# Transposing keys and queries by the DMA crossbar instead of by matmuls, in an attention kernel fused with a gated long convolution

## Chip, core and metric

The kernel runs on one core of one Trainium2 chip. The metric is the device time of one execution in microseconds (us); lower is better. Every run has a span (first to last instruction). A single run over 1.5% above the fastest of its kernel counts as slow and is left out of ratios.

## The reference

For 4 batches, 8 heads, 768 positions and a head dimension of 64, each query attends to the 8 first keys and to the 96 last ones, with a slope per head. The result, as a [768 x 512] matrix per batch, is projected to three parts; the second is convolved over the whole sequence, multiplied with the other two, and projected once more.

```python
scores = scale * q @ k.T                  # kept: key < 8, or 0 <= query - key < 96
a = softmax(scores - slope[h] * dist)
x = heads_side_by_side(a @ v)             # [B, 768, 512]
x1, x2, x3 = split(x @ w_proj)
y = x1 * irfft(rfft(x2) * rfft(filter)) * x3
out = y @ w_out                           # float32
```

## The kernel before

The engines' names: PE is TensorE's matmul, PEld its weight load, DVE VectorE, ACT ScalarE, POOL GpSimd, SP SyncE. Keys lie in seven tiles of 128 rows: the 8 global keys, then 120 local ones. POOL issues the loads (float32 to float16 on the way); SP issues a small copy that repeats the 8 global rows in all seven tiles, and the output stores.

```python
def load_tiles(self, dst, src, b):                       # keys or values
    g.dma_start(dst[0:NG, 0, :, 0:D], src[b, :, 0:NG, :]...)
    self.nc.sync.dma_start(dst[0:NG, 1:7], dst[0:NG, 0:1].to_broadcast(...))   # by SP
    for t in range(7):
        g.dma_start(dst[NG:P, t, :, 0:D], src[b, :, lo:lo + KL, :]...)         # by POOL

def load_batch(self, b):
    qt, kt, vt = self.batch_tiles()      # natural layout, two buffers of each
    self.load_tiles(kt, self.k, b)
    for t in range(6):
        g.dma_start(qt[:, t], self.q[b, :, P * t:P * t + P, :]...)
    self.load_tiles(vt, self.v, b)
    if b == 1: ...                       # gate parts of w, then w_out
```

Scores need head dimensions on the partitions. So for each pair of heads PE transposes six blocks of queries and seven of keys against an identity; ACT copies the queries' result out of PSUM, DVE the keys'.

```python
def transpose_k(self, hp, kt, first):    # branch for batches 1 to 3
    for m in range(7):
        nc.tensor.transpose(tk[:, P * m:P * m + P], kt[:, m, hs, :], self.ident)
    nc.vector.tensor_copy(KT, tk[:, 0:7 * P])

def weights(self, hp, gi, QT, KT):       # scores of one pair, one of three groups
    sp = self.ps.tile([P, 2, 512], F32, tag="s", bufs=1)    # a single PSUM buffer
    ...                                  # matmuls of KT and QT into sp
    nc.scalar.activation(eo, sp[...], Act.Exp, scale=self.scale)
```

`weave` records the attention of batch b+1 and the rest (called hyena: projections, transforms, gates, output) of batch b in turns, chunk by chunk. Each engine then runs its instructions in the recorded order. The matmuls meant to keep PE's clock up in batch 0 are idle ones (`busy`).

The softmax here doesn't subtract the row's maximum and nothing guards it: scores larger than these inputs give would overflow.

## Time and profile before

The median was 212.75 us (212.4 to 213.83, four runs). I divide the span at the first matmul of each hyena, the accumulation of the weights' middle part with `xa`:

| stretch of the profile before | from, us | length, us |
|---|---|---|
| batch 0's attention, filter, tables | 0 | 46.08 |
| first middle stage: hyena 0 and attention 1 | 46.08 | 43.17 |
| second middle stage | 89.25 | 43.04 |
| third middle stage | 132.29 | 42.70 |
| last stage: hyena 3 alone | 174.99 | 35.01 |

In order of time PE's row looks so at the start of the second middle stage. The columns are start and length in us, engine, line, operation, output<-inputs, shapes and count; a bracket gives the idle time before and what ended it:

```profile
85.67 3.40 PE L661 MATMUL pt<-wo,y 128*128 128x512 f16 x15
88.91 0.50 PE L466 MATMUL tr<-ident,qt 128*128 128x128 f16 x6
89.25 1.03 PE L579 MATMUL pt<-w,xa 128*128 128x512 f16 x4
90.45 0.55 PE L491 MATMUL tr<-ident,kt 128*128 128x128 f16 x7 [0.18 <-ACT QT L471]
...
91.80 0.36 PE L503 MATMUL sp<-QT,KT 64*128 64x216 f16 x4
```

PE goes from the output projection (`wo`) into the next stage without a gap: the transposes of the new batch stand between matmuls of the other stream, and the first scores (`sp`) come at 91.80. The loads are far ahead. POOL waited 15.0 us for a values buffer before it began batch 3's loads at 83 us, for a stage that starts at 132.

### The profile page before, as it was taken

The page shows a single profiled execution, that of the slowest core. Times are in us where ns is not written, and L with a number is a line of the kernel's source. Part 1 is how long each engine was busy: PE and PEld are TensorE (multiplying, and loading weights), DVE is VectorE, ACT ScalarE, POOL GpSimd, SP SyncE. Part 2 cuts the span into 40 slices and gives each one's busy share as a digit, 9 for nine tenths or more (in the row PEclk, how much of TensorE's full clock was granted, in tenths as well). Part 3 has the DMA queues.
Part 4 walks back from the last instruction along what each step waited for, and adds up shares of the span by engine and source line. Part 5 has one row for each costly group of instructions (what it writes and reads, how often), then busy time and mean ns, then how long its engine had stood idle before and what let it go on. Part 6 is the DMA issues. An engine that isn't in the chain of part 4 may idle for free.

```text
span 210.0 us, 4253 instructions
## 1 busy us (share of the span) xinstructions
PE 189.5 (90%) x1661; PEld 102.7 (49%) x1661; DVE 147.0 (70%) x328; ACT 149.7 (71%) x243; POOL 75.6 (36%) x102
## 2 busy tenths in 40 slices
PE   7587888679899999998999999989999999998981
PEld 2233454345465656444555664535565654454630
DVE  5965899973499999332999995147998960196820
ACT  6997985436797785769786866787859856665642
POOL 7999459995699001996810000000000000000000
PEclk9999999999999999999999999999999999999998
DMA  5999999999999900999990003500000025000034
GB/s 190 167 124 189 205 154 155 126 142 207 158 157 137 81 3 0 147 235 184 143 97 2 3 2 116 186 0 3 0 0 3 2 100 203 0 0 0 3 118 185
DMA packets 79629, 20.62 MB, mean 98 GB/s; under 512 B 71336, under 2 KB 76536, under 8 KB 79608
## 3 DMA queue, kind: packets, MB, share of 16 engines
q0 software_dynamic: 74672, 12.13, 91.8%
q1 hardware_dynamic: 4936, 8.21, 11.6%
q8 instruction: 13, 0.21, 0.4%
q14 instruction: 8, 0.07, 0.1%
HBM read 25.79 MB, written 6.29 MB: 153 GB/s over the span
## 4 chain that ended last, share of the span: by engine, by line
DVE 48%; PE 29%; ACT 8%; issue 5%; DMA 5%; POOL 3%; POOLq 0%; DVEq 0%
DVE xn L540 9%; PE pt L661 7%; PE pt L579 7%; DVE g L570 6%; PE pt L565 4%; DVE E_107 L522 3%; DMA t<-in_k_dram 3%; DMA vt<-in_v_dram 2%; DVE E_107 L519 2%; PE tr L547 2%; DVE rc L539 2%; ACT E_104 L510 2%; DVE y L651 2%; PE tr L491 2%; PE pt L643 2%
## 5 line engine op out<-in xcount | busy, mean ns | idle before, releaser
L565 PE MATMUL pt<-xT,w 128*128 128x384 f16 x256 | 46.5, 327 | 0.0
L565 PEld LDWEIGHTS <-w 128*128 128x128 f16 x256 | 23.3, 98 | 15.9 <-issue 1.6
L107 POOL DMA_DIRECT2D vt<-in_v_dram x28 | 25.7, 944 | 1.4 <-DMA qt<-in_q_dram 0.8
L510 ACT ACTIVATE E_107<-sp 128x864 f16<-128x864 f32 x24 | 21.5, 897 | 2.7 <-PE sp L503 2.7
L510 ACT ACTIVATE E_104<-sp 128x864 f16<-128x864 f32 x24 | 21.6, 899 | 2.2 <-PE sp L503 1.9
L664 ACT ACTIVATE t<-pt 128x512 f32<-128x512 f32 x24 | 14.3, 598 | 12.0 <-PE pt L661 11.8
L107 POOL DMA_DIRECT2D kt<-in_k_dram x21 | 19.0, 915 | 10.3 <-DMA fl<-in_moe_filter_fft_dram 4.2
L503 PE MATMUL sp<-QT,KT 64*128 64x216 f16 (+2 forms) x224 | 17.8, 250 | 5.4 <-ACT E_104 L510 2.5
L661 PE MATMUL pt<-wo,y 128*128 128x512 f16 x96 | 22.0, 379 | 0.7 <-DVE y L654 0.7
L540 DVE TENSOR_TENSOR xn<-o,rc 128x448 f16<-128x448 f32 x32 | 20.0, 624 | 1.1
L548 ACT COPY xT<-tr 128x768 f16<-128x768 f16 x16 | 12.8, 797 | 9.4 <-PE tr L547 9.4
L643 PE MATMUL pt<-inv,X 128*128 128x384 f16 x96 | 18.4, 326 | 0.9 <-DVE X L604 0.9
L503 PEld LDWEIGHTS <-KT 64*128 64x128 f16 x224 | 7.7, 95 | 23.5 <-issue 19.8
L581 ACT CAST dst<-pt 128x512 f16<-128x512 f32 x24 | 14.3, 596 | 6.8 <-PE pt L579 6.8
L327 PE MATMUL pt<-dst,fwd 128*128 128x512 f16 x72 | 18.8, 379 | 0.0
L607 ACT CAST X<-pt 128x512 f16<-128x512 f32 x24 | 14.1, 589 | 6.4 <-PE pt L327 6.0
L522 DVE TENSOR_TENSOR E_104<-E_104,mask 128x864 f16<-128x864 f16 x16 | 9.6, 603 | 9.7 <-ACT E_104 L510 8.8
L115 POOL DMA_DIRECT2D qt<-in_q_dram x18 | 15.9, 903 | 1.3 <-DMA kt<-in_k_dram 1.3
L279 PE MATMUL pt<-idle 128*128 128x512 f16 x35 | 15.1, 436 | 1.3 <-DVE warm L688 1.2
L661 PEld LDWEIGHTS <-y 128*128 128x128 f16 x96 | 8.8, 98 | 10.9 <-DVE y L654 2.1
L492 DVE COPY KT<-tr 128x896 f16<-128x896 f16 x12 | 7.4, 618 | 7.7 <-PE tr L491 7.7
L579 PE MATMUL pt<-w,xa 128*128 128x512 f16 x48 | 12.2, 380 | 0.3 <-DVE xa L450 0.3
(234 smaller groups left out, 370.4 us busy)
## 6 DMA issues: line engine op xcount, KB each, us to landing
out_dram<-t SPq DMA_DIRECT2D x24, 256.0 KB, 2.4
vt<-in_v_dram POOLq DMA_DIRECT2D x28, 120.0 KB, 6.5
kt<-in_k_dram POOLq DMA_DIRECT2D x21, 120.0 KB, 9.1
qt<-in_q_dram POOLq DMA_DIRECT2D x18, 128.0 KB, 5.7
w<-in_moe_w_proj_dram POOLq DMA_DIRECT2D x3, 512.0 KB, 8.0
t<-in_q_dram SPq DMA_DIRECT2D x2, 384.0 KB, 5.8
t<-in_k_dram SPq DMA_DIRECT2D x2, 384.0 KB, 5.6
fl<-in_moe_filter_fft_dram POOLq DMA_DIRECT2D x1, 768.0 KB, 11.9
```

The lines of the kernel that those rows point to most:

```text
L107: g.dma_start(dst[NG:P, t, :, 0:D], src[b, :, lo:lo + KL, :].rearrange("h p d -> p h d"))
L115: g.dma_start(qt[:, t], self.q[b, :, P * t:P * t + P, :].rearrange("h p d -> p h d"))
L279: self.nc.tensor.matmul(pt, self.idle[:, 0:P], self.idle, start=True, stop=True)
L327: self.nc.tensor.matmul(pt, self.fwd[:, kt, s, :], src[:, kt, :], start=(kt == 0), stop=(kt == 2))
L503: nc.tensor.matmul(sp[:, hh, off:off + w], KT[64 * hh:64 * hh + 64, o:o + P], QT[64 * hh:64 * hh + 64, KL * m:KL * m + w], start=(off == 0 ...
L510: nc.scalar.activation(eo, sp[:, :, 0:432].rearrange("p h (m w) -> p h m w", m=2), Act.Exp, scale=self.scale)
L522: nc.vector.tensor_mul(eo, eo, mk[:, :, 0:2] if gi == 0 else mk[:, :, 1:3])
L540: nc.vector.tensor_mul(xn[:, :, hh, :], o[:, :, 0:D], rc.to_broadcast([P, 7, D]))
L565: nc.tensor.matmul(pt[:, 0:h], self.w[:, c, o + P * j:o + P * j + P], xT[:, c, h * s:h * s + h], start=(c == 0), stop=(c == 3))
L579: nc.tensor.matmul(pt, src[:, c, P * t:P * t + P], self.w[:, c, DM:2 * DM], start=(c == 0), stop=(c == 3))
L643: nc.tensor.matmul(pt[:, 0:h], X[:, s, cs], self.inv[:, s, :], start=(s == slots[0]), stop=(s == slots[-1]))
L661: nc.tensor.matmul(pt, y[:, c, P * t:P * t + P], self.wo[:, c, :], start=(c == 0), stop=(c == 3))
```

## The change

The keys of batches 1 to 3 and the queries of 2 and 3 are to be transposed by the crossbar of the DMA, SBUF to SBUF, issued by SP. PE, DVE and ACT lose the work; nothing on them takes its place. The natural keys and queries now have one buffer each instead of two, since the room goes to whole transposed tiles. The queries of batch 1 stay with PE, because the DMA is full at that time (9 tenths busy up to 73 us in the profile before).

```diff
+LATE = 26
+GATES = (1, 0, 0, 0, 1, 0, 3)
     def load_batch(self, b):
+        kt = self.ld.tile([P, 7, H, D], F16, tag="k", bufs=1)
+        qt = self.ld.tile([P, 6, H, D], F16, tag="q", bufs=1)
         self.load_tiles(kt, self.k, b)
         for t in range(6):
             g.dma_start(qt[:, t], self.q[b, :, P * t:P * t + P, :]...)
+        KT, QT = self.transposed_tiles()
+        if b == 1:
+            self.QT1, QT = QT, None
+        def transposed():
+            self.nc.sync.dma_start_transpose(KT..., kt...)          # 28 blocks of 128x128
+            for t in range(6 if QT is not None else 0):
+                self.nc.sync.dma_start_transpose(QT[:, :, t], qt[:, t]...)   # 4 blocks each
+        vt = self.batch_tiles()
+        if b == 1:
+            transposed()
+        else:
+            self.after(LATE, transposed)        # recorded 26 chunks later
         self.load_tiles(vt, self.v, b)
@@ attention: no key transposes, query transposes only for batch 1
-                             (i + 1 < n, lambda: trk(i + 1)),
+                             (i + 1 < n and first, lambda: trk(i + 1)),
-                             (i + 1 < n, lambda: trq(i + 1)),
+                             (i + 1 < n and (first or natural), lambda: trq(i + 1)),
@@ ... batch 0's scratch moves into these tiles; the weave's chunk counts become 29 and 25
```

More of the change, by code (lines that the diff above doesn't have):

```diff
@@ L92, in batch_tiles @@
         D = self.D
-        qt = self.ld.tile([P, 6, self.H, D], F16, tag="q")
-        kt = self.ld.tile([P, 7, self.H, D], F16, tag="k")
         vt = self.ld.tile([P, 7, self.H, D + 1], F16, tag="v")
         self.nc.gpsimd.memset(vt[:, :, :, D:D + 1], 1.0)
-        return qt, kt, vt
+        return vt
     def load_tiles(self, dst, src, b):
@@ L108, in load_tiles, with transposed_tiles @@
                         src[b, :, lo:lo + KL, :].rearrange("h p d -> p h d"))
+    def transposed_tiles(self):
+        KT = self.ld.tile([P, 7, self.H // 2, P], F16, tag="KT")
+        QT = self.ld.tile([P, self.H // 2, 6, P], F16, tag="QT")
+        return KT, QT
     def load_batch(self, b):
         g = self.nc.gpsimd
-        qt, kt, vt = self.batch_tiles()
+        H, D = self.H, self.D
+        kt = self.ld.tile([P, 7, H, D], F16, tag="k", bufs=1)
+        qt = self.ld.tile([P, 6, H, D], F16, tag="q", bufs=1)
         self.load_tiles(kt, self.k, b)
@@ L115, in load_batch @@
             g.dma_start(qt[:, t], self.q[b, :, P * t:P * t + P, :].rearrange("h p d -> p h d"))
+        KT, QT = self.transposed_tiles()
+        if b == 1:
+            self.QT1, QT = QT, None
+        def transposed():
+            self.nc.sync.dma_start_transpose(KT.rearrange("c t a p -> c (t a) p"),
+                                             kt.rearrange("p t h d -> p (t h d)"))
+            for t in range(6 if QT is not None else 0):
+                self.nc.sync.dma_start_transpose(QT[:, :, t],
+                                                 qt[:, t].rearrange("p h d -> p (h d)"))
+        vt = self.batch_tiles()
[3 more added lines that the diff above has]
+            self.after(LATE, transposed)
         self.load_tiles(vt, self.v, b)
@@ L120, in load_batch @@
             self.load_w_out()
-        return qt, kt, vt
+        return QT if QT is not None else qt, KT, vt
     def load_first(self):
@@ L142, in cast_first @@
         for src in (sq, sk):
-            t = self.mp.tile([P, 6, P], F16, tag=f"c{len(out)}", name="t")
+            t = self.cst[:, hp % 2, len(out)]
             self.nc.vector.tensor_copy(t.rearrange("p t (h d) -> p t h d", h=2),
@@ L377, in filter_spectrum, with attention @@
             yield 1
-    def attention(self, qt, kt, vt, xT, xa, xb, first=None):
+    def attention(self, qt, kt, vt, xT, xa, xb, first=None, natural=False):
         n = self.H // 2
         qk, cst = {}, {}
+        if not first:
+            qk = {i: {0: None if natural else qt[:, i].rearrange("c t p -> c (t p)"),
+                      1: kt[:, :, i]} for i in range(n)}
         def trq(i):
-            if i < n:
-                qk.setdefault(i, {})[0] = self.transpose_q(i, cst[i][0] if first else qt, first)
+            qk.setdefault(i, {})[0] = self.transpose_q(i, cst[i][0] if first else qt, first)
         def trk(i):
-            if i < n:
-                qk.setdefault(i, {})[1] = self.transpose_k(i, cst[i][1] if first else kt, first)
+            qk.setdefault(i, {})[1] = self.transpose_k(i, cst[i][1])
         def sc(i, g):
@@ L422, in attention @@
             cst[0], ths = first
-        trq(0)
-        if first:
+            trq(0)
             for a in (2, 3):
                 self.dft_sines(a, ths[a][0])
-        yield 1
-        trk(0)
-        cast(1)
-        yield 1
+            yield 1
+            trk(0)
+            cast(1)
+            yield 1
+        elif natural:
+            trq(0)
+            yield 1
         for i in range(n + 1):
             for live, fn in ((i < n, lambda: sc(i, 0)),
-                             (i + 1 < n, lambda: trk(i + 1)),
+                             (i + 1 < n and first, lambda: trk(i + 1)),
                              (i < n, lambda: sc(i, 1)),
                              (i > 0, lambda: val(i - 1, 0)),
-                             (i + 1 < n, lambda: trq(i + 1)),
+                             (i + 1 < n and (first or natural), lambda: trq(i + 1)),
                              (i > 0, lambda: val(i - 1, 1)),
@@ L460, in transpose_q @@
         nc, S = self.nc, self.S
-        hs = slice(2 * hp, 2 * hp + 2)
-        QT = self.ap_.tile([P, S], F16, tag="qT")
         tq = self.tr(first)
-        src = qt if first else qt[:, :, hs, :]
-        for st in range(6):
-            nc.tensor.transpose(tq[:, P * st:P * st + P], src[:, st], self.ident)
         if first:
+            QT = self.qk[:, hp % 2, 7 * P:]
+            for st in range(6):
+                nc.tensor.transpose(tq[:, P * st:P * st + P], qt[:, st], self.ident)
             nc.scalar.copy(QT.rearrange("c (p r) -> c p r", r=6),
@@ L470, in transpose_q, with transpose_k @@
         else:
+            QT = self.QT1[:, hp].rearrange("c t p -> c (t p)")
+            for st in range(6):
+                nc.tensor.transpose(tq[:, P * st:P * st + P], qt[:, st, 2 * hp:2 * hp + 2, :],
+                                    self.ident)
             nc.scalar.copy(QT, tq[:, 0:S])
         return QT
-    def transpose_k(self, hp, kt, first):
+    def transpose_k(self, hp, kt):
         nc, S = self.nc, self.S
-        hs = slice(2 * hp, 2 * hp + 2)
-        KT = self.ap_.tile([P, 7 * P], F16, tag="kT")
-        tk = self.tr(first)
-        if first:
-            for st in range(6):
-                nc.tensor.transpose(tk[:, P * st:P * st + P], kt[:, st], self.ident)
-            tv = tk[:, 0:S].rearrange("c (r p) -> c p r", r=6)
-            kv = KT.rearrange("c (t j) -> c t j", t=7)
-            loc = kv[:, :, NG:].rearrange("c t (p r) -> c t p r", r=6)
-            nc.vector.tensor_copy(loc[:, 0:6], tv[:, 0:KL].rearrange("c (t p) r -> c t p r", t=6))
-            nc.vector.tensor_copy(loc[:, 6], tv[:, P - 20:P])
-            nc.vector.tensor_copy(kv[:, :, 0:NG],
-                                  kv[:, 0:1, NG:2 * NG].to_broadcast([P, 7, NG]))
-        else:
-            for m in range(7):
-                nc.tensor.transpose(tk[:, P * m:P * m + P], kt[:, m, hs, :], self.ident)
-            nc.vector.tensor_copy(KT, tk[:, 0:7 * P])
+        KT = self.qk[:, hp % 2, 0:7 * P].rearrange("c (t p) -> c t p", t=7)
+        tk = self.tr(True)
+        for st in range(6):
+            nc.tensor.transpose(tk[:, P * st:P * st + P], kt[:, st], self.ident)
+        tv = tk[:, 0:S].rearrange("c (r p) -> c p r", r=6)
+        loc = KT[:, :, NG:].rearrange("c t (p r) -> c t p r", r=6)
+        nc.vector.tensor_copy(loc[:, 0:6], tv[:, 0:KL].rearrange("c (t p) r -> c t p r", t=6))
+        nc.vector.tensor_copy(loc[:, 6], tv[:, P - 20:P])
+        nc.vector.tensor_copy(KT[:, :, 0:NG],
+                              KT[:, 0:1, NG:2 * NG].to_broadcast([P, 7, NG]))
         return KT
@@ L500, in weights @@
         for m in self.GRP[gi]:
-            w, o = self.EW[m], P * m
+            w = self.EW[m]
             for hh in range(2):
                 nc.tensor.matmul(sp[:, hh, off:off + w],
-                                 KT[64 * hh:64 * hh + 64, o:o + P],
+                                 KT[64 * hh:64 * hh + 64, m, :],
                                  QT[64 * hh:64 * hh + 64, KL * m:KL * m + w],
@@ L615, in more @@
             return js
-        if more():
-            yield 1
-        for s in range(6):
-            self.forward(s, ab[0], ab[1], evac)
-            yield 1
-            if s % 2 == 1 and s > 1 and more():
-                yield 1
-        for _ in range(2):
-            if more():
+        for s, k in enumerate(GATES):
+            for _ in range(k):
+                if more():
+                    yield 1
+            if s < 6:
+                self.forward(s, ab[0], ab[1], evac)
                 yield 1
@@ L701, in emit @@
         self.distances()
-        qkv = self.batch_tiles()
+        vt = self.batch_tiles()
+        KT, QT = self.transposed_tiles()
+        self.qk = KT.rearrange("c t a p -> c (t a p)")[:, 0:26 * P].rearrange(
+            "c (i x) -> c i x", i=2)
+        self.cst = QT.rearrange("c a t p -> c (a t p)").rearrange(
+            "p (i k t c) -> p i k t c", i=2, k=2, t=6)
         self.fwd = cp.tile([P, 3, 6, P], F16)
@@ L710, in emit @@
             self.dft_sines(a, ths[a][0])
-        self.load_tiles(qkv[2], self.v, 0)
+        self.load_tiles(vt, self.v, 0)
         self.load_pairs(2, nc.gpsimd, F16)
@@ L715, in emit @@
         x = self.new_x()
-        self.weave((self.attention(*qkv, *x, first=(cast, ths)), 34, 0, 1),
+        self.weave((self.attention(None, None, vt, *x, first=(cast, ths)), 34, 0, 1),
                    (self.filter_stage(), 10, 0.7, 1))
-        loads = [qkv, self.load_batch(1)]
+        loads = [None, self.load_batch(1)]
         for b in range(self.B):
@@ L725, in emit @@
                 nx = self.new_x()
-                streams.insert(0, (self.attention(*loads[b + 1], *nx), 34,
+                streams.insert(0, (self.attention(*loads[b + 1], *nx, natural=b == 0), 29 if b == 0 else 25,
                                    0.0, 0.9))
```

## The prediction

> **What bounds the kernel now.** I read the page from the top (busy shares, the 40 slices), then the chain that ended last in order of time, then the busy time by stage. The page says that no single engine is idle enough to be ruled out:
>
> ```profile
> PE 189.5 (90%) x1661; PEld 102.7 (49%) x1661; DVE 147.0 (70%) x328; ACT 149.7 (71%) x243; POOL 75.6 (36%) x102
> PE   7587888679899999998999999989999999998981
> DVE  5965899973499999332999995147998960196820
> DMA  5999999999999900999990003500000025000034
> ```
>
> The kernel has five stages. Batch 0's attention fills 0 to 46 us. Then come three near-identical stages, in which the hyena part of batch b and the attention of batch b+1 are woven together: in the chain, the first line of the weave (the accumulation "PE pt L579") follows the copy "ACT QT L471" at 46, 90 and 133 us, so the period is 43.05 us. The last stage, hyena of batch 3 alone, is 175 to 210. The change touches only the three middle stages. The second of them, cut in three (columns: stretch, its length, busy time of PE, PEld, DVE, ACT and POOL, then granted clock, DMA share, GB/s):
>
> ```profile
> 90.00:98.00 8.00, 7.24 (x60) 3.36 (x57) 2.64 (x6) 6.34 (x11) 6.29 (x8) 1.00 1.89 218
> 98.00:128.00 30.00, 29.69 (x307) 17.31 (x303) 27.58 (x60) 22.32 (x39) 6.46 (x8) 1.00 1.14 52
> 128.00:133.00 5.00, 4.90 (x33) 2.67 (x34) 1.07 (x3) 3.89 (x7) 0.00 (x0) 1.00 0.61 226
> ```
>
> The reader is to see two regimes. In the 30 us in the middle DVE is busy 27.6 us, and the chain runs along it almost without a break; in the 13 us at the two ends DVE does little and PE is full, with ACT close behind at the start (6.34 of 8).
>
> Busy PE time overstates PE, because neighbouring matmuls overlap. So I take the step from one matmul to the next in runs of one group: 8 gate matmuls in 1.47 us with a last one of 0.327 make (1.47-0.33)/7 = 0.163 us each; in the same way 0.216 for the 512-wide ones, 0.164 for L643, 0.055 for a 128x128 transpose (7 in 0.55, one lasting 0.219), 0.032 for the value matmuls. For one stage: L565 64x0.163 = 10.4, L579 5.2, L327 3.9, L643 3.9, L661 5.2, values 104x0.032 plus small gaps 3.9, twelve score groups at 0.39 (from the end of the matmuls before to the next group) 4.7, transposes of x 1.5, of keys 28x0.055 = 1.5, of queries 24x0.055 = 1.3. The sum is 41.5 of 43.05 us. **PE is within about 1.5 us of being the bound of every middle stage**, and DVE is nearly full for two thirds of it. A change must relieve both to gain much, and this one does.
>
> **What the Trainium skill says.** "Trace Analysis" is not needed beyond what the skill's entry page, "Trainium Kernel Development and Optimization", says under its Performance Expectations: matmul busy time is a bad metric since matmuls are pipelined. The trace agrees: 219 ns for one transpose, 55 ns from one to the next. "VectorE: DVE Perf Modes", section "The three transpose paths", gives 390 ns for a 128x128 transpose on TensorE and 1309 ns by the DMA crossbar. TensorE's figure is far above the 55 ns step here; for the crossbar no run before has a number. "DMA: Bandwidth & Descriptors", section "Latency and other measured facts", gives the DMA transpose 261 GB/s for a non-contiguous middle dimension and 350 to 400 GB/s contiguous. The same page, "Issuing engines are not separate DMA queues", says that transfers from all issuers share the same 16 DMA engines and interleave; so transposes issued by SP will share with the loads issued by POOL. The slices agree that sharing matters: DMA is at 9 tenths up to 73 us.
>
> **The change part by part.** The rows that it concerns:
>
> ```profile
> L491 PE MATMUL tr<-ident,kt 128*128 128x128 f16 x84 | 6.6, 219 | 0.4 <-ACT QT L471 0.4
> L466 PE MATMUL tr<-ident,qt 128*128 128x128 f16 x72 | 6.0, 219 | 0.1
> L492 DVE COPY KT<-tr 128x896 f16<-128x896 f16 x12 | 7.4, 618 | 7.7 <-PE tr L491 7.7
> L471 ACT COPY QT<-tr 128x768 f16<-128x768 f16 x12 | 9.6, 801 | 1.5 <-PE tr L466 1.5
> ```
>
> Removed: all 84 key transposes and 48 of the 72 query transposes (the order of the changed program has 132 fewer matmuls on PE), the 12 DVE copies and 8 of the 12 ACT copies. The gate order given by GATES is the same as the loop that it replaces had: one gate first, one before the fifth forward group, three after the last. So the last stage is unchanged, and so is batch 0, whose scratch tiles only move into others. For a stage with both removed (two of them): PE loses 1.5+1.3 = 2.8 us, DVE 4x0.618 = 2.5, ACT 4x0.801 = 3.2. For the first middle stage, only keys: PE 1.5, DVE 2.5.
>
> How much of that is on the path? In the DVE-bound middle lie two of the four key copies (109.05 and 100.69 in the second stage), so about 1.25 us less; PE's two query and two key transposes there are 1.4 us, about the same, so the stretch shortens by some 1.25 us. At the ends, PE-bound, the other 1.4 us of transposes go, but they were also what PE did while the scores waited: the scores' PSUM buffer exists once, so a score group must wait until ACT's exponential of the group before is done: about 0.6 us to the start and 0.90 us of work. Before, the groups that had only one 4-matmul chunk between them were 1.9 us apart, with 0.58 us of PE wait. After, more of them stand like this (the order shows scores, one L579 chunk, scores, four times running), and ACT's exponential and cast, 0.90+0.59 us per pair, set about 1.5 us a step against PE's 0.39+0.86 = 1.25. I estimate that a bit under half of the 1.4 us returns as this wait, leaving 0.8. The removed start of the stage (query copy, key transposes, key copy, 89.7 to 91.8 us on the chain) lets scores start earlier and is worth perhaps 0.45 more. **Full stage: 1.25+0.8+0.45 = 2.5 us; two of them 5.0.**
>
> First middle stage: 1.25 on DVE and about 0.25 on PE, 1.5 in all, less what the loads cost. The key transfer is 28 blocks of 32 KB, 0.92 MB: 3.5 us at the skill's 261 GB/s (an estimate from that page), twice that beside loads that fill the DMA, and some 2 us of latency. Keys of batch 1 are issued until 29.7 us and take 9 to 11 us to land, so the transposes start near 40 and end at 46 to 49; the first scores stood at 48.8 and would now come near 47. The loads behind them (parts of w, landed at about 52, used at 55) come 3 or 4 us later. I charge 0.7 us. **First stage: 0.8 us.**
>
> Sum: 5.0+0.8 = 5.8; 213.06-5.8 = 207.3 us.
>
> **The rivals.** (1) The crossbar is slow. At 1309 ns a block without overlap, the keys of a batch would take 37 us and its queries 31. For batch 2 the keys land near 60 and the stage starts near 88, so the queries would be ready at about 125 and each full stage would wait some 30 us: 250 us or more. For it speaks that figure of the skill; against it the bandwidth figures of the other page, and that 1309 ns looks like one block's latency, not a rate. At a third of the good bandwidth (keys 10 us, queries 8) batches 2 and 3 are still hidden, because their loads land 10 us or more ahead, and only batch 1 would be late, by about 5 us: then the total is near 211 to 212. (2) PE's relief turns into waits for ACT: if all that PE saves at the ends returns, a full stage gains only 1.25, and the total is about 210. For it speaks the single score buffer and ACT's 6.34 of 8 us. (3) Everything comes through: the whole 2.8 us of PE in two stages, 1.5 in the first, and some of the old waits too: 205 or a little under. For it speaks that all three engines lose work and that PE was at 41.5 of 43. (4) A serialized SP queue: transposes wait on loads with output stores behind them; six staging buffers hold the outputs. The transposes stand well ahead of the stores (about 80 against 84.6 us), so I expect nothing.
>
> **Range and chances.** Central 207.3; 203.5 if rival 3 and a little more happens, 211 if batch 1's keys are late or rival 2 holds fully. The 2% line is 208.8, 1.5 us above the centre, with a spread of some 3 us: faster 0.68, within 2% 0.27, slower (rival 1) 0.05.
>
> **What would show each step.** The period of the second and third middle stages should fall from 43.05 to about 40.5; the first from 43.9 to about 43. DVE and ACT busy should fall by about 7.4 and 6.4 us, PE's count by 132. The wait of score matmuls on ACT's exponentials should rise from 0.6 us a stage to 1.5 or more. DMA transposes of keys should take 4 to 8 us. The prediction is wrong if the first scores of a stage wait for a transposed tile for over 2 us, if gates wait for w, or if the middle of a stage doesn't shorten although DVE has less to do.

## The result

The changed kernel took 215.34 us (215.06 to 215.99, four runs) against 212.75. A ratio in this document is the mean time of one kernel's fast runs over that of the other's of the same rounds, so it is not quite the ratio of the medians. Here it is 1.0117, interval 1.0071 to 1.0164: 1.2% slower, where 2.7% faster had been predicted. On another chip, the same kernel gave 1.0093 (1.0039 to 1.0147).

These are the rows of the page of the changed kernel that answer to those of before, in 40 slices of the span, with the granted clock (PEclk) added:

```profile
PE 187.8 (88%) x1529; PEld 99.2 (46%) x1529; DVE 141.7 (66%) x316; ACT 143.8 (67%) x235; POOL 76.1 (36%) x102
PE   7486988798789999958998999999899999998982
DVE  5964799973238989711479998426799961187630
PEclk9997899969969999996999999999999999999999
DMA  6999999999999599999999996530000007000025
```

The work did go: 132 matmuls fewer, DVE 5.3 us and ACT 5.9 us less busy (7.4 and 6.4 had been predicted). But PE now has a weak slice from 91 to 96 us (a 5, with DVE at 1). The clock, at 9 up to the last slice before, shows a 6 in three slices (43 to 48, 59 to 64, 96 to 102 us) and a 7 and an 8 from 16 to 27 us, and the DMA is busy at 9 tenths till 128 us, but for one slice. Where PE waited, from the view of waits (engine, line, what for; then us in total, times, longest), beginning with the changed kernel:

```profile
PE sp L525 <- ACT E_104 L532: 4.0, 9, 1.0
PE sp L525 <- DMA QT<-qt: 2.9, 1, 2.9
PE pt L587 <- DMA w<-in_moe_w_proj_dram: 2.3, 2, 1.7
...
PE sp L525 <- DMA KT<-kt: 0.5, 1, 0.5
```

and before:

```profile
PE sp L503 <- ACT E_104 L510: 2.5, 5, 0.6
```

Before, no matmul of PE waited for a DMA in this view. After, three kinds do. The stages say where it went:

| stretch | before, us | after, us | difference |
|---|---|---|---|
| batch 0 | 46.08 | 47.70 | +1.6 |
| first middle stage | 43.17 | 49.88 | +6.7 |
| second middle stage | 43.04 | 41.98 | -1.1 |
| third middle stage | 42.70 | 39.91 | -2.8 |
| last stage | 35.01 | 34.63 | -0.4 |

The gain is there, in full in the third stage, and the first stage gives back more. PE's row at its two places, in order of time, first the gates of batch 0:

```profile
56.36 0.36 PE L525 MATMUL sp<-QT,KT 64*128 64x216 f16 x4
57.27 0.82 PE L587 MATMUL pt<-xT,w 128*128 128x384 f16 x4 [0.55 <-DMA w<-in_moe_w_proj_dram]
59.80 1.24 PE L587 MATMUL pt<-xT,w 128*128 128x384 f16 x4 [1.70 <-DMA w<-in_moe_w_proj_dram]
```

and the passage into the second stage:

```profile
91.32 2.75 PE L680 MATMUL pt<-wo,y 128*128 128x512 f16 x12
97.00 0.65 PE L525 MATMUL sp<-QT,KT 64*128 64x216 f16 x4 [2.92 <-DMA QT<-qt]
97.58 3.58 PE L601 MATMUL pt<-w,xa 128*128 128x512 f16 x8
```

At 57 us PE waits for the gate parts of `w`. POOL issued them 3.4 and 5.2 us later than in the trace before, since it waited for loads in flight, and each landed 11.9 us after its issue (7.7 and 9.5 before). At 94 us PE waits 2.9 us for transposed queries. Then eight matmuls take 3.58 us, 0.43 us each, twice the 0.216 of a PE at full clock; the granted clock from 97.58 to 101.20 us is 0.53 on the mean. The Trainium skill, "TensorE: Matmul & The Clock Gate", Part 1, describes this: after an idle window of about 3.4 us the array runs at half clock until it has been busy about as long. The trace agrees on the half clock and on its length: each of the four low stretches of this profile lasts 3.4 us. It does not agree on the idle time. This wait was 2.9 us, and at 60.0 us the clock fell after waits of only 0.55 and 1.70 us, with PE busy for 1.16 of the last 3.4. Nor does every short wait do it: in after_again, a repeat of this kernel described below, waits of 0.33 and 1.18 us at the same place left the clock full.

Why were the queries late? SP's and POOL's rows in order of time:

```profile
62.47 0.69 SPq L103 DMA_DIRECT2D kt<-kt  x1
80.35 0.69 SPq L103 DMA_DIRECT2D vt<-vt  x1
81.39 7.76 SPq L128 DMA_TRANSPOSE KT<-kt  x1
89.25 8.59 SPq L131 DMA_TRANSPOSE QT<-qt  x6
97.93 1.00 SPq L684 DMA_DIRECT2D out_dram<-t  x2
```

```profile
71.48 5.29 POOL L122 DMA_DIRECT2D qt<-in_q_dram  x6 [8.02 <-PE tr L498]
76.71 0.42 POOL L96 MEMSET vt<- 128x56 f16 x1
77.79 0.61 POOL L102 DMA_DIRECT2D vt<-in_v_dram  x1 [0.66 <-POOL vt L96]
```

Read this backwards. The query transposes stand behind the key transposes, whose issue alone holds SP for 7.8 us. These stand behind the repetition of the values' global rows (`vt<-vt`), for which SP had waited 17 us. The values are loaded after the queries, and the query load waited 8.0 us for PE's last query transposes of batch 1 (L498), because the natural queries have one buffer. So a matmul at 71 us decided when keys that had long been loaded could be transposed.

This gave the theory for the experiments. **Theory A:** the gain per stage is real, and is hidden by two waits and by the clock lost after them. One is for `w`, pushed back by the crossbar's share of the DMA. The other is for batch 2's queries, held by the order of the instructions on SP and POOL. **Rival B:** the crossbar beside loads is so slow that no order helps. **Rival C:** only the wait for `w` matters, or it was the chip.

### The profile page after: what moved, and what is told of

The parts are those of the page before. It is cut to its first block, busy times and chain, and to the rows that moved or that the text cites.

```text
span 214.1 us, 3993 instructions
## 1 busy us (share of the span) xinstructions
PE 187.8 (88%) x1529; PEld 99.2 (46%) x1529; DVE 141.7 (66%) x316; ACT 143.8 (67%) x235; POOL 76.1 (36%) x102
## 4 chain that ended last, share of the span: by engine, by line
PE 43%; DMA 22%; DVE 14%; ACT 7%; POOL 7%; issue 4%; SPq 2%; POOLq 0%; DVEq 0%; ACTq 0%
PE pt L587 13%; DMA vt<-in_v_dram 8%; PE pt L601 7%; PE pt L680 7%; PE pt L350 6%; DMA w<-in_moe_w_proj_dram 6%; DMA fl<-in_moe_filter_fft_dram 5%; DVE g L592 3%; PE sp L525 3%; PE pt L662 3%; DMA QT<-qt 3%; PE tr L569 2%; POOL qt L122 2%; ACT E_104 L532 2%; DVE xn L562 2%
## 5 line engine op out<-in xcount | busy, mean ns | idle before, releaser
L587 PE MATMUL pt<-xT,w 128*128 128x384 f16 x256 | 47.2, 328 | 2.6 <-DMA w<-in_moe_w_proj_dram 2.3
L680 PE MATMUL pt<-wo,y 128*128 128x512 f16 x96 | 22.7, 379 | 1.5 <-DVE y L673 1.5
L525 PEld LDWEIGHTS <-KT 64*128 64x128 f16 x224 | 8.6, 94 | 30.0 <-issue 22.7
L350 PE MATMUL pt<-dst,fwd 128*128 128x512 f16 x72 | 19.6, 391 | 0.0
L544 DVE TENSOR_TENSOR E_104<-E_104,mask 128x864 f16<-128x864 f16 x16 | 9.7, 605 | 14.1 <-ACT E_104 L532 13.2
L525 PE MATMUL sp<-QT,KT 64*128 64x216 f16 (+2 forms) x168 | 13.2, 243 | 6.4 <-DMA QT<-qt 2.9
L302 PE MATMUL pt<-idle 128*128 128x512 f16 x35 | 15.8, 457 | 1.3 <-DVE warm L707 1.2
L601 PE MATMUL pt<-w,xa 128*128 128x512 f16 x48 | 13.6, 422 | 0.3 <-DVE xa L476 0.3
L544 DVE TENSOR_TENSOR E_107<-E_107,mask 128x864 f16<-128x864 f16 x16 | 9.6, 603 | 5.6 <-ACT E_107 L532 5.6
## 6 DMA issues: line engine op xcount, KB each, us to landing
w<-in_moe_w_proj_dram POOLq DMA_DIRECT2D x3, 512.0 KB, 11.9
```

The lines of the kernel that those rows point to most:

```text
L302: self.nc.tensor.matmul(pt, self.idle[:, 0:P], self.idle, start=True, stop=True)
L350: self.nc.tensor.matmul(pt, self.fwd[:, kt, s, :], src[:, kt, :], start=(kt == 0), stop=(kt == 2))
L525: nc.tensor.matmul(sp[:, hh, off:off + w], KT[64 * hh:64 * hh + 64, m, :], QT[64 * hh:64 * hh + 64, KL * m:KL * m + w], start=(off == 0), ...
L544: nc.vector.tensor_mul(eo, eo, mk[:, :, 0:2] if gi == 0 else mk[:, :, 1:3])
L587: nc.tensor.matmul(pt[:, 0:h], self.w[:, c, o + P * j:o + P * j + P], xT[:, c, h * s:h * s + h], start=(c == 0), stop=(c == 3))
L601: nc.tensor.matmul(pt, src[:, c, P * t:P * t + P], self.w[:, c, DM:2 * DM], start=(c == 0), stop=(c == 3))
```

## The experiments

Twelve runs were made, each on one chip with the kernel before run beside them. Diffs are against the changed kernel unless said otherwise.

| run | median us | ratio to before | middle stages in its profile, us |
|---|---|---|---|
| changed kernel, first result | 215.34 | 1.0117 | 49.9, 42.0, 39.9 |
| kfirst | 211.51 | 0.9962 | 46.3, 40.7, 39.9 |
| wearly | 219.90 | 1.0310 | (slow profile) |
| b1pe | 216.86 | 1.0191 | 46.1, 45.7, 39.9 |
| warm | 211.13 | 0.9929 | (slow profile) |
| gatelate | 213.10 | 0.9964 | 45.3, 41.7, 39.9 |
| earlyq | 210.99 | 0.9903 | 46.1, 40.3, 39.9 |
| all3 | 209.12 | 0.9773 | (slow profile) |
| quiet | 214.12 | one look | 49.6, 41.4, 39.9 |
| after_again | 214.69 | 1.0093 | 48.7, 42.0, 39.9 |
| warm_again | 213.29 | 1.0017 | 47.3, 40.3, 39.9 |
| all4 | 207.24 | 0.9739 | 43.2, 40.3, 39.9 |
| b1pe2 | 209.45 | 0.9838 | 44.4, 40.9, 39.9 |

The third stage is 39.9 us in every profile, the slow ones too: what the change does to a stage in which PE waits for no DMA repeats in each run. The 95% intervals of the ratios reach 0.5 to 1.0% to each side. By them only all4 is clearly over 2% faster and wearly over 2% slower; all3, b1pe and b1pe2 stay unclear by that measure, and the others are within 2% of before. Medians of different calls should not be compared; the kernel before had 212.06, 214.08 and 213.04 us in the three calls.

### kfirst: keys ahead of the values' repetition on SP

```diff
-            self.nc.sync.dma_start_transpose(KT..., kt...)      # out of transposed()
...
+        self.nc.sync.dma_start_transpose(KT..., kt...)
         vt = self.batch_tiles()
-        if b == 1:
-            transposed()
-        else:
-            self.after(LATE, transposed)
+        self.after(LATE, transposed)
         self.load_tiles(vt, self.v, b)
```

> Change: SP issues the key transposes of batches 2 and 3 before the broadcast of the values' first rows, instead of after it. Theory A (SP's order: the key transposes of batch 2 stood behind a broadcast that waits for the values, which wait for the queries' single buffer): the keys are issued near 72 us instead of 81.4, the scores of batch 2 no longer wait 2.9 us for QT, PE stays warm, and the time falls by 3 to 5 us from 215.3 to about 211. Rival B (the transposes cost DMA time, and whoever issues them earlier only slows the loads of queries and values beside them): QT lands as late as before or later, time within 1 us of 215.3. Rival C (all of it is the first middle stage's wait for w): no change.

Keys were issued at 68.3 us instead of 81.4, the wait for queries fell to 0.45 us, and the eight matmuls at the start of the stage, which now come ahead of it, took 1.90 us. The ratio went from 1.0117 (or 1.0093) to 0.9962, some 3 us. This speaks for the order on SP and against Rival B. The waits for `w` stayed at 0.32 and 1.60 us.

### wearly: w before the values of batch 1

```diff
-        self.load_tiles(vt, self.v, b)
         if b == 1:
             for part in (0, 2):
                 self.load_w_in(part)
+        self.load_tiles(vt, self.v, b)
+        if b == 1:
             self.load_w_out()
```

> Change: the two gate parts of w for batch 0 are loaded before the values of batch 1. Theory A (key transposes of batch 1 push the loads behind them back by some 7 us, and w is the one that is missed): the gate waits of 2.3 us go, but the values of batch 1 now land last, near 60 us, and their first use near 58 us waits instead; net gain 0 to 2 us, about 214. Rival C (only w matters and the values have slack): gain 3 us or more with the lost warm clock, about 212. If the queue order is all that matters later (batch 2), nothing changes at 97 us.

A miss. It was 3.1% slower than before, with 217.8 us in its best run. Its profile (a slow run, 223.3 us, so only a hint for its sizes) has a wait that nobody had expected:

```profile
60.84 0.54 PE L526 MATMUL sp<-QT,KT 64*128 64x216 f16 x4 [12.63 <-DMA KT<-kt]
```

The keys of batch 1, issued at 34.1 us as in the changed kernel, took 26.7 us to land instead of 15.8, with the two 512 KB loads of `w` now beside them. So in this profile the loads beside them made the transposes later in their turn, and moving a load forward did not make room.

### warm and warm_again: idle matmuls in the wait

```diff
+        elif self.warm2:                 # once, for batch 2
+            self.warm2 = False
+            self.busy(12)
         for i in range(n + 1):
```

> Change: 12 idle matmuls (2.6 us of PE at full clock) ahead of the first scores of batch 2, in the time in which PE waits for QT. Theory A (the wait itself costs 2.9 us, and the lower granted clock after it another 1.7 us, seen as 3.6 instead of 1.7 us for the eight matmuls that follow): the eight take 1.7 to 2 us and the time falls by 1 to 2 us, to about 213.8. Rival (the clock has its own window and would be low anyway, or the idle matmuls delay the scores): no change or 0.5 us slower.

The first run came out 4 us below the changed kernel's first result, more than expected, but without that kernel on the same chip. So both were run side by side, five rounds each:

> The changed kernel unaltered, as the reference for the others of this call on the same chip. Theory A: about 1.01 of before, 213 to 216 us, with waits for w (about 2.3 us) and QT (about 3 us) and one or two stretches of lower clock as in the first profile. If it came out 2% below before, the first result would have been the chip's.

> The 12 idle matmuls ahead of batch 2's first scores, beside the unaltered change on the same chip. Theory A (the wait for QT costs about 3 us and the lower granted clock after it some 1.7 us more): 1 to 2 us below after_again, and the eight matmuls after the wait at 1.9 us. Rival (the first gain of 4 us against the other chip's runs was the chip): within 0.7 us of after_again.

The changed kernel repeated its result (1.0093). With the idle matmuls it was 213.29 against 214.69 us, 1.4 us less, which fits the 1.7 us by which the eight matmuls exceed 1.9. (By the means it is 1.8 us, with a 95% interval of about 0.5 to 3.1, so the size is rough.) The profile of warm_again shows the eight at 1.90 us, after the idle matmuls and a remaining wait for QT of 0.5 us. The lost clock is a cost of its own; the rest of the first 4 us did not repeat.

### b1pe: batch 1 wholly by matmuls

```diff
 # against kfirst
-        kt = self.ld.tile([P, 7, H, D], F16, tag="k", bufs=1)
+        kt = self.ld.tile([P, 7, H, D], F16, tag="k", bufs=2)
-        self.nc.sync.dma_start_transpose(KT..., kt...)
+        if b == 1:
+            self.KT1, KT = KT, None
+        else:
+            self.nc.sync.dma_start_transpose(KT..., kt...)
-        t = self.mp.tile([P, 768], dt, tag="stg", bufs=6)
+        t = self.mp.tile([P, 768], dt, tag="stg", bufs=5)
 # ... and trk(i + 1) for batch 1 as before the change
```

> Change: batch 1 wholly by matmuls as before the change (keys in two natural buffers, five staging tiles instead of six to make room), with the key transposes of batches 2 and 3 ahead of the broadcast as in kfirst. Theory A: the first middle stage takes 43 to 44 us again, without waits for w or KT, the two later ones 40 each: 210.0 - 2x2.9 in span, so about 207 in time, the number that the prediction had without its first stage. Rival B (crossbar transposes slow whatever runs beside them, or their queue order still makes QT late): the scores of batch 2 wait again, 209 to 212. If five staging tiles hurt, output copies wait for stores.

Slower than expected, but its profile tells the parts apart. Up to the wait for queries its first stage ran without any wait for a DMA, and PE reached that wait at 89.9 us, 43.2 us after the stage's start, as before the change: the wait for `w` does come from the key transposes of batch 1. After that the queries were late by 1.5 and 0.9 us, and then the output copies stopped, in ACT's row:

```profile
89.07 0.60 ACT L692 ACTIVATE t<-pt 128x512 f32<-128x512 f32 x1 [0.27 <-PE pt L689]
97.42 0.60 ACT L692 ACTIVATE t<-pt 128x512 f32<-128x512 f32 x1 [7.76 <-DMA out_dram<-t]
```

The stores stood on SP behind the query transposes (81.0 to 90.4 us), and with five staging tiles the sixth output had no place. Being issued late was not all: two of these stores have a recorded landing, 8.2 and 8.6 us after issue, where the median of the run is 2.0, and in this stage of the kernel before it is 3.6. In the changed kernel the stores were issued from 97.9 us, and no output copy waited for them: its six tiles hold the six outputs.

### gatelate, earlyq, all3

The first gate of batch 0 after three forward groups:

```diff
-        for s, k in enumerate(GATES):
+        for s, k in enumerate(GATES if b else (0, 0, 0, 1, 1, 0, 3)):
```

> Change: in batch 0's hyena the first gate is computed after three forward groups instead of before them; nothing else, so w is needed some 3 to 4 us later. Theory A (the key transposes of batch 1 delay w by about 7 us, and the gate's wait for it costs 2.3 us plus about 1 us at a lower granted clock): the wait for w goes, batch 0's stage shortens by 2.5 to 3.5 us; but the scores of batch 2 still wait for QT, whose loads are tied to the last query transposes of batch 1, so that wait grows unless these come earlier too: total 2 to 3.5 us below the changed kernel, about 212.5 where that has 215.3. Rival (the stage is full anyway): within 1 us.

No gate waited for `w` any more. The first stage took 45.3 us, 4.6 less than in the first profile of the changed kernel and 3.3 less than in the second one. The wait for queries stayed (2.90 us). The ratio is 0.9964, 1.3 to 1.5% or about 3 us below the changed kernel's two of the other calls.

All query transposes of batch 1 at the start of its attention, on top of kfirst:

```diff
         elif natural:
-            trq(0)
-            yield 1
+            for i in range(n):
+                trq(i)
+                yield 1
```

> Change: kfirst, and all four query transposes of batch 1 stand at the start of its attention, so that the single natural query buffer is free near 52 us and not 71. Theory A (queue order and the single buffer tie QT of batch 2 to the last query transposes): POOL issues the queries of batch 2 right after its keys, near 63 us, QT is issued by 80 us and no score of batch 2 waits; 0.5 to 1.5 us below kfirst (211.5), about 210.5. Rival B (transposes slow the loads): the wait stays, no gain. The gate's wait for w stays about as it is or is smaller by what PE now does before it.

POOL issued the queries of batch 2 at 62.6 us instead of 71.5, right after the keys, and no score waited for them. The waits for `w` stayed, 0.37 and 1.70 us. The ratio, 0.9903 against kfirst's 0.9962, lies in the direction expected, but the intervals overlap, so the times alone do not show this step's gain. A simpler cure, a second buffer for queries, does not build: it is 1 KB per partition short.

All three together:

> Change: kfirst, early query transposes of batch 1, and the later first gate of batch 0 together. Theory A (two waits and the lost warm clock hid the gain): all three middle stages near 40 to 42 us, no wait of PE for a transposed tile or w over 0.5 us, total about 207 (205.5 to 208.5), that is the number of the prediction. Rival (something else takes its place, such as ACT or the score buffer): 209 or more.

The ratio was 0.9773, and the median of 209.12 us is no longer the 205.5 to 208.5 of Theory A: it falls to the rival that something is left. The profile, a slow run of 211.57 us, still had one wait for a later block of queries, 1.81 us. SP issued them from 81.0 us though POOL had issued their loads by 69.5: they still stood behind the values' repetition.

### all4: queries too ahead of the values' repetition

```diff
 # against all3; spread() is the repetition of the 8 global rows
-        self.load_tiles(vt, self.v, b)
+        self.load_tiles(vt, self.v, b, spread=b == 1)
+        if b > 1:
+            self.after(LATE, lambda: self.spread(vt))      # recorded after the transposes
```

> Change: all3, and SP issues the query transposes of batches 2 and 3 before the broadcast of the values too, so that no transpose waits for a later load. Theory A (order on SP): queries are issued as they land, near 77 to 86 us; no score of batch 2 waits (1.8 us in all3's profile); 1 to 2 us below all3's 209.1, ratio to before 0.965 to 0.972. Rival (the crossbar beside the value loads is what is slow): the wait stays near 1.8 us, same time as all3.

207.24 us (206.5 to 208.43), ratio 0.9739 (0.9692 to 0.9787), and 7.4 us below the changed kernel of the same call. SP's row, and PE's at the passage into the second stage:

```profile
67.59 6.40 SPq L136 DMA_TRANSPOSE KT<-kt  x1
74.09 11.52 SPq L133 DMA_TRANSPOSE QT<-qt  x6
85.72 0.71 SPq L111 DMA_DIRECT2D vt<-vt  x1
```

```profile
86.97 2.75 PE L684 MATMUL pt<-wo,y 128*128 128x512 f16 x12
89.65 0.36 PE L529 MATMUL sp<-QT,KT 64*128 64x216 f16 x4
89.94 1.90 PE L605 MATMUL pt<-w,xa 128*128 128x512 f16 x8
```

Keys go at 67.6 us, queries from 74.1 us, PE passes without a gap, and the granted clock of the profiled run is 1.0. PE waits for no DMA at all. This is the best version found. Against all3 the ratio fell by only 0.3%, less than the 1 to 2 us expected, and the intervals overlap; that the last step helped is shown by the order on SP and by the missing wait, not by the times.

### b1pe2: the order of all4 with batch 1 by matmuls

Its edits are those of b1pe, early query transposes, and the order of all4 on SP; its gates stay early.

> Change: batch 1 wholly by matmuls, with the order of all4 on SP, early query transposes of batch 1 and five staging tiles; its gates stay early. Theory A (the crossbar for batch 1 is worth only 1.5 us of PE and costs 7 us of DMA time ahead of w): no wait for w, first middle stage 43.2 as before the change, the two others near 40: within 1.5 us of all4, ratio 0.968 to 0.978, and 6 us or more below b1pe, whose stores stood behind the query transposes. Rival (five staging tiles are what cost b1pe): output copies wait for stores again by several us.

209.45 us, by the ratios 3.5% or 7 us below b1pe, and 2.2 us above all4 (1.1%), where within 1.5 us had been expected: a miss. One output copy waited for a store, 1.2 us instead of 7.8, although it has five staging tiles as well. So five tiles alone did not cost b1pe its 7 us; they did together with stores that stood behind the query transposes. The 2.2 us against all4 may mean that the crossbar for batch 1's keys pays once its side effects are gone. That is not shown: the order of gates and the staging differ between the two as well.

### quiet: the crossbar alone

```diff
+            if b == 3:
+                # batch 3's keys again, without a reader: once as 28 blocks, then 7 times 4
+                nc.sync.dma_start_transpose(KX..., self.kt3...)
+                for t in range(7):
+                    nc.sync.dma_start_transpose(KY[:, t], self.kt3[:, t]...)
```

> Change: the changed kernel, with batch 3's keys transposed two times more in the last stage, when no loads run: once as one transfer of 28 blocks, once as seven of 4. Measures the crossbar by itself. Prediction's estimate (skill's 261 GB/s plus 2 us): 28 blocks land in 5.5 us. If SP's issue sets the pace (0.28 us a block in the changed kernel): issue near 7 to 8 us and landing near 9. If the engines do: landing near 15 us as with loads beside it. The extra transposes have no reader and should change the time by less than 1 us.

SP's row, then the DMA's traffic from 176 to 206 us in 40 slices of 0.75 us:

```profile
178.84 4.49 SPq L756 DMA_TRANSPOSE KX<-kt  x1
183.43 9.06 SPq L760 DMA_TRANSPOSE KY<-kt  x7
```

```profile
GB/s 66 194 382 382 330 209 220 217 218 218 217 162 82 153 23 174 45 130 103 72 157 20 172 0 0 0 0 0 0 0 0 0 22 0 0 0 0 0 0 317
```

The first slices, at 382 GB/s, are output stores. Then the 28 blocks run at a steady 217 to 220 GB/s until about 184.5 us. The profile has no landing for this transfer; by the traffic it ended between 5 and 6 us from its issue, and the prediction's estimate of 5.5 fits. The seven pieces take twice the time on SP, 1.3 us each. Beside loads, the same 28 blocks needed 15.8 us for batch 1, and 7.1 to 7.9 us of SP in the first profile of the changed kernel (4.3 to 8.4 in the others, but for wearly's 14.7). So the crossbar by itself is as fast as expected; what was wrong was the price of company. This is one profiled run.

## Why the prediction was wrong

It named 207.3 us, range 203.5 to 211; the result was 215.3 and slower. Two of the signs that it had named for being wrong came: scores that wait over 2 us for a transposed tile (2.9) and gates that wait for `w` (2.3). Step by step:

- **What bounds the kernel, and the gain of a full stage: right.** 2.5 us were predicted; the third stage fell by 2.8, and the second, in all4, by 2.75. The predicted score wait on ACT's exponential came in part: from 0.6 us before to 1.0 in the third stage (two waits, 0.8 the longest), where 1.5 or more had been named. The 43.9 us that it read for the first stage came from uneven marks (45.8 to 89.7); by the first matmul of each stage it was 43.17.
- **"I charge 0.7 us" for the loads of the first stage: too small.** The key transfer was put at 3.5 us alone, "twice that beside loads", 46 to 49 us. It landed at 49.7, 15.8 us after its issue at 33.9 (the estimate had started it near 40). Above all it pushed `w` back by 7.6 us and not 3 or 4: the second gate part landed at 59.8, where the trace before saw it landed at 52.2. PE waited 2.3 us for it, and the next matmuls ran at the low clock. That waiting is gone in gatelate and, without the transfer, in b1pe.
- **"A serialized SP queue ... I expect nothing": the step that failed most.** The prediction asked only whether the transposes delay the stores behind them. It never asked what stood in front of them. Their own place, behind the values' repetition, behind the values' load, behind a single query buffer, made them late by 3 us (4.5 in the second profile of the changed kernel). The prediction had them stand at "about 80" us; the keys' transposes were issued at 81.4, and those of the queries held SP until 97.8. Slow landing is part of it: the keys landed 14.8 us after their issue, at 96.2. In all4 they took as long (14.6 us), but issued at 67.6 they were there by 82.2. kfirst, earlyq and all4 removed the links of the order one by one. The order was in the built program and could have been read before.
- **The clock after a wait: not thought of.** 1.7 us in the profile after the wait for queries, 1.4 in the side-by-side runs.
- **The first stage's own gain of 1.5 us: not seen.** Even in all4, without a wait for a DMA, that stage took 43.23 us, as before the change (43.17). PE waited there 1.2 us for ACT in its score groups instead of 0.6; the rest stays open. b1pe2, where the keys come by PE, took 44.4 with a similar arrangement, so some gain may be eaten by the early query transposes; no run isolates this.
- **Batch 0: +1.6 us in the first profile.** Matmuls of the same code ran at a lower clock there. In later profiles this part ended between 46.6 and 48.8 us for kernels that agree up to there, so it varies from run to run. The clock is not all of it: profiles without a low stretch in this part ended it between 46.6 and 48.4. The rest stays open.

That all4 came out at 207.24, next to the predicted 207.3, is partly luck: the sum had 0.8 us for a first stage that gave none, and a little less for the others than they gave.

## What to carry to other kernels

When work moves from an engine to a DMA queue, write down everything that stands before it on the issuing engine, and each of those transfers' own waits for buffers, and compare with the time at which its reader needs it. A transfer on a full DMA also delays the others (here `w`, by 7.6 us), so ask who else is just in time. And a short wait of PE costs more than itself when it lets the clock fall (here 1.7 us on top of 2.9).

## What the Trainium skill lacked or had wrong

- "DMA: Bandwidth & Descriptors", section "Latency and other measured facts": 261 GB/s for a transpose with a non-contiguous middle dimension, 350 to 400 contiguous; alone, this ran at 217 to 220 GB/s, below both. No page gives a figure for a transpose beside loads in small packets: 15.8 us instead of 5 to 6 for 0.92 MB, and 7.6 us of delay for a load behind it.
- "DMA: Bandwidth & Descriptors", "Issuing engines are not separate DMA queues": it calls the sequencer's time to issue usually small against the DMA. Here a transpose of 28 blocks held SP for 4.5 us alone, most of its 5 to 6 us to land, and for 7.1 to 7.9 us beside loads in the first profile of the changed kernel, half of its time to land. What stood behind transposes waited: in b1pe an output copy for 7.76 us. No page warns that transposes on the queue of the stores delay these.
- "VectorE: DVE Perf Modes", "The three transpose paths": 1309 ns for one block by the crossbar reads like a rate; 28 blocks in 5 to 6 us are some 0.2 us each, and four blocks landed in 2.5 us. Its 390 ns for TensorE stands against a step of 55 ns from one transpose to the next here.
- "TensorE: Matmul & The Clock Gate", Part 1: the half clock (eight matmuls at 0.43 us each) and its 3.4 us agree. The idle window of about 3.4 us before it does not: here the clock fell after single waits of 2.92 and 1.70 us, the latter with PE busy for a third of the 3.4 us before, and stayed full after others of 1.2 us. The page does not say how much work within a window keeps the clock.
